# Splitting the first layernorm statistics between ScalarE and VectorE at the start of a fused attention and MLP kernel

## The chip, the cores and the metric

The kernel runs on one core of one Trainium2 chip. The metric is the device time of the whole program in microseconds (us), the median of several runs. All ratios below are the mean time of one kernel's fast runs over the mean of the other's fast runs of the same rounds, so they are not quite the ratio of the medians that stand beside them. "Span" is the length of the one profiled execution; it is some 2 us shorter than the time of the same run.

## The reference, cut to what matters

Two residual blocks on x of 2048 tokens by 1024 columns, in bf16: a linear-memory attention, then a gated MLP. The change touches only the first line of the first block, for the first 512 tokens.

```python
h  = x + _A_ref(_layernorm(x, axis=-1), A_wq, A_wk, A_wv, A_wo, A_beta)
h2 = h + _B_ref(_layernorm(h, axis=-1), B_w_in, B_w_sp, B_b_sp, B_w_out)

def _layernorm(x, axis=-1, eps=1e-05):
    m = jnp.mean(x, axis=axis, keepdims=True)
    v = jnp.var(x, axis=axis, keepdims=True)
    return (x - m) / jnp.sqrt(v + eps)
# ...
    v = (x @ wv).reshape(B, S, H, Dh) ...   # the first products the kernel makes
```

## The kernel before

The program records every operation with the tiles it reads and writes. A list scheduler in the source then fixes the order on each engine from a rough duration for each operation, and semaphores are set from the dependencies. So each engine's order is static: an instruction that waits for a late load holds up all that stand behind it on its engine (below, 0.59 us on VectorE in the changed kernel).

The start loads four x chunks of 128 tokens (x0 to x3, x0 in two halves of 512 columns) and wv in three pieces. The comments in the cut below are added here. The letters of `LOAD` are the order of issue after x0: x1, x2, rows 0 to 3 of wv's first 512 columns ("a"), rows 4 to 7 of the same ("b"), x3, and the other 512 columns ("h"). "Row" here means one block of 128 rows.

```python
    N_WARM = 11                      # matmuls on zeros, before any data is there
    ON_ACT = (1,)                    # x1's statistics are taken on ScalarE
    LOAD = "12ab3h"
    START = 'T00 t01 v00 v01 v02 v03 t10 T11 v04 v05 v06 v07 v10 v11 v12 v13 v14 T20 T21 v15 ...'
    AFTER = [(1, 1, 5)]
    # ...
    def layernorm_act(src, dst, junk, k):          # x1, all 1024 columns on ScalarE
        nm, ss = MV[k][:, 0:1], MV[k][:, 1:2]
        G.op(ACT, lambda e: e.activation(junk, src, ACTF.Identity, scale=-1.0 / D, accum_out=nm), ...)
        G.op(ACT, lambda e: e.activation(junk, src, ACTF.Square, bias=nm, accum_out=ss), ...)
        act(RS[k][:], ss, ACTF.Sqrt, scale=1.0 / D, bias=EPS[:])
        recip(RS[k][:], RS[k][:])
        ts(dst, src, nm, RS[k][:], ALU.add, ALU.mult)
```

`START` is TensorE's order. `T00` or `t00` turns (transposes on TensorE) the first four column blocks of x0; the evictions of a capital T go to VectorE, those of a small t to ScalarE. `v04` is the product of x0's column block 4 with row 4 of wv, first 512 columns; `u04` the same for the other 512. `v00` to `v03` need only the first piece of wv, "a", and the turn `T00`. `v04` to `v07` need piece "b". x3 is turned by a transposing DMA. `AFTER` is one order constraint more: x1's square pass on ScalarE waits until x0 is normalized.

The softmax here doesn't subtract the row's maximum and nothing guards it: scores larger than these inputs give would overflow.

Of the kernel before, what the change touches and what calls it, by code (L numbers as in the profile page):

```python
# [10 lines left out]
ACTF = mybir.ActivationFunctionType  # L11
ALU = mybir.AluOpType

T = 2048
D = 1024
# [8 lines left out]
LN_EPS = 1e-5  # L24
MEM_EPS = 1e-6

PE, ACT, DVE, POOL, SP = range(5)
# [319 lines left out]
def bass_sequential_preLN__memory_aug_infini_attn__mixer_gmlp__prompt_kernel(  # L347
# [16 lines left out]
    G = _Prog(nc)  # L364
# [13 lines left out]
    def tens(name, shape, dt, off=None):  # L378
        sz = int(np.prod(shape[1:])) * mybir.dt.size(dt)
        if off is None:  # L380
            off = region(sz)
        assert off % 32 == 0 and off + sz <= ARENA, (name, off, sz)
        t = nc.alloc_sbuf_tensor_at(name, list(shape), dt, offset=abase + off)
        G.base[t.name] = off
        return t
# [20 lines left out]
    XIN = [tens("xin%d" % i, [128, D], BF16, R_XIN + i * 2048) for i in range(4)]  # L406
    R_HX = region(8192)
    HX = [tens("hx%d" % i, [128, D], BF16, R_HX + i * 2048) for i in range(4)]
# [15 lines left out]
    G1 = tens("g1", [128, H], F32)  # L424
# [3 lines left out]
    MHALF = tens("mhalf", [128, 1], F32)  # L428
    EPS = tens("eps", [128, 1], F32)
    STATS = [tens("stats%d" % i, [128, 4, 6], F32) for i in range(4)]  # L430
    MV = [tens("mv%d" % i, [128, 4], F32) for i in range(4)]
    RS = [tens("rs%d" % i, [128, 1], F32) for i in range(4)]
# [2 lines left out]


    N_WARM = 11
    ON_ACT = (1,)
    LOAD = "12ab3h"


    START = 'T00 t01 v00 v01 v02 v03 t10 T11 v04 v05 v06 v07 v10 v11 v12 v13 v14 T20 T21 v15 v16 v17 v20 v21 v22 v23 v24 v25 v26 v27 u00 u01 u02 u03 u04 u05 u06 u07 u10 u11 u12 u13 u14 u15 u16 u17 u20 u21 u22 u23 u24 u25 u26 u27 v30 v31 v32 v33 v34 v35 v36 v37'
    AFTER = [(1, 1, 5)]
    PS = nc.alloc_psum_tensor("ps", [128, 8, 512], F32)
    G.psum = PS.name

# [3 lines left out]
    def n_of(ap):  # L450
        return int(np.prod([x[1] for x in list(ap.ap)[1:]]))

    def inps(ap):
        return ap.tensor.name == PS.name
# [15 lines left out]
    def act(o, i, func, scale=1.0, prio=0, bias=None):  # L470
        r = [i] + [x for x in (scale, bias) if x is not None and not isinstance(x, float)]
        kw = {} if bias is None else {"bias": bias}
        G.op(ACT, lambda e: e.activation(o, i, func, scale=scale, **kw), r, [o],  # L473
             ((172 if inps(i) else 224) + n_of(i)) / 1.2 + 26, prio=prio, name=str(func))

    def vcost(o, ins, fast):
        n = n_of(o)
        if any(inps(x) for x in ins):
            return ((n / 2 if ins[0].dtype == BF16 and len(ins) == 1 else n) + 151) / 0.96
        if fast == 1:  # L480
            return (n + 151) / 0.96
        return (n / fast + (268 if fast == 4 else 151)) / 0.96
# [4 lines left out]
    def ts(o, i, s1, s2, op0, op1, fast=4):  # L487
        r = [i] + [s for s in (s1, s2) if not isinstance(s, float)]
        G.op(DVE, lambda e: e.tensor_scalar(o, i, s1, s2, op0, op1), r, [o], vcost(o, [i], fast), name="ts", prio=late[0])  # L489
# [11 lines left out]
    def recip(o, i):  # L501
        G.op(DVE, lambda e: e.reciprocal(o, i), [i], [o], (8 * n_of(o) + 151) / 0.96, name="recip", prio=late[0])  # L502

    def ptt(o, a, b, op):
        G.op(POOL, lambda e: e.tensor_tensor(o, a, b, op), [a, b], [o], 550 if op == ALU.pow else
             200 + 1.8 * n_of(o), name="ptt", prio=late[0])

    def pts1(o, i, s, op):
        G.op(POOL, lambda e: e.tensor_single_scalar(o, i, s, op), [i], [o], 220 if n_of(o) < 8 else 220 + 2.5 * n_of(o), name="pts1", prio=late[0])  # L509
# [14 lines left out]
    def bank():  # L524
        b = bank_set[0][bank_rr[0] % len(bank_set[0])]
        bank_rr[0] += 1
        return PS[:, b, :]
# [12 lines left out]
    def w_half(W, A, h, after=False):  # L540
        dma(W[:, :, h * 512:(h + 1) * 512], A.rearrange("(c p) n -> p c n", p=128)[:, :, h * 512:(h + 1) * 512],
            after=after)
# [16 lines left out]

    ln_rr = [0]  # L560

    def layernorm(src, dst, w, prio=0, start=False):
        late[0] = prio
        k = ln_rr[0] % 4
        ln_rr[0] += 1
        nch = (w + 511) // 512
        cs = w // nch
        for ci in range(nch):
            si, so = src[:, ci * cs:(ci + 1) * cs], STATS[k][:, ci, :]
            G.op(DVE, lambda e, si=si, so=so: e.bn_stats(so, si), [si], [so], (cs + 143) / 0.96, name="bn_stats",  # L570
                 prio=late[0])
        sa, mv = STATS[k][:, 0:nch, :], MV[k][:, 0:2]
        G.op(DVE, lambda e: e.bn_aggr(mv, sa), [sa], [mv], 210, name="bn_aggr", prio=late[0])  # L573
        if start:
            act(RS[k][:], MV[k][:, 1:2], ACTF.Sqrt, bias=EPS[:])
            recip(RS[k][:], RS[k][:])
        else:
            pts1(RS[k][:], MV[k][:, 1:2], LN_EPS, ALU.add)
            ptt(RS[k][:], RS[k][:], MHALF[:], ALU.pow)
        ts(dst, src, MV[k][:, 0:1], RS[k][:], ALU.subtract, ALU.mult)  # L580
        late[0] = 0

    def layernorm_act(src, dst, junk, k):
        nm, ss = MV[k][:, 0:1], MV[k][:, 1:2]
        G.op(ACT, lambda e: e.activation(junk, src, ACTF.Identity, scale=-1.0 / D, accum_out=nm), [src], [junk, nm],  # L585
             1250, name="sum")
        G.op(ACT, lambda e: e.activation(junk, src, ACTF.Square, bias=nm, accum_out=ss), [src, nm], [junk, ss],  # L587
             1250, name="sumsq")
        act(RS[k][:], ss, ACTF.Sqrt, scale=1.0 / D, bias=EPS[:])
        recip(RS[k][:], RS[k][:])  # L590
        ts(dst, src, nm, RS[k][:], ALU.add, ALU.mult)


    NJ = [512, 384, 256, 128]
# [13 lines left out]
    def x_load(tc):  # L608
        dma(XIN[tc % 4][:], x2d[tc * 128:(tc + 1) * 128, :])

    def x_norm(tc):
        layernorm(XIN[tc % 4][:], XIN[tc % 4][:], D, 600)

    def x_turn_pe(tc, h, eng):
        dst = XNT[0][:, :, tc * 128:(tc + 1) * 128]
        bb = bank().bitcast(BF16)
        for i in range(4):
            c = 4 * h + i
            tr(bb[:, i * 128:(i + 1) * 128], XIN[tc][:, c * 128:(c + 1) * 128])
        bv = bb[:, 0:512].rearrange("p (c n) -> p c n", c=4)  # L620
        if eng == DVE:
            late[0] = -200
            copy(dst[:, 4 * h:4 * h + 4, :], bv)
            late[0] = 0
        else:
            act(dst[:, 4 * h:4 * h + 4, :], bv, ACTF.Copy)

    def x_turn(tc):
        s, tcl = divmod(tc, 4)
        dma(XNT[s % 2][:, :, tcl * 128:(tcl + 1) * 128], XIN[tc % 4][:], transpose=True)  # L630
# [164 lines left out]
    for i in range(2):  # L795
        pset(V[i][:, :, :, 32:34], 1.0)
    bank_rr[0] = 0
    first = []
    for tcl in range(4):
        first.append(len(G.ops))  # L800
        if tcl in ON_ACT:
            layernorm_act(XIN[tcl][:], XIN[tcl][:], HX[tcl % 2][:], (tcl + 2) % 4)
        else:
            layernorm(XIN[tcl][:], XIN[tcl][:], D, start=True)
    turned, vb = {}, {}
    x_turn(3)
    w_half(WK, A_wk, 0)
    G.ops[-1].deps.add(first[3] + 5)
    for x in START.split():
        c, i = int(x[1]), int(x[2])  # L810
        if x[0] in "tT":
            x_turn_pe(c, i, DVE if x[0] == "T" else ACT)
            turned[c, i] = len(G.ops) - 1
            continue
        if i == 0:
            vb[x[:2]] = bank()
        b, h = vb[x[:2]], x[0] == "u"
        mm(b[:], XNT[0][:, i, c * 128:(c + 1) * 128], WV[:, i, 512 * h:512 * h + 512], i == 0, i == 7)
        if i == 7:
            act(V[0][:, c, 16 * h:16 * h + 16, 0:32], b.rearrange("p (h d) -> p h d", d=32), ACTF.Copy)  # L820
        if x == "u27":

            G.op(ACT, lambda e: e.activation(G1[:, 0:1], RS[2][:], ACTF.Exp, scale=0.0), [RS[2][:]], [G1[:, 0:1]],
                 1500, name="table")

    for c, k, d in AFTER:
        G.ops[first[c] + k].deps.add(turned[d] if isinstance(d, tuple) else first[d // 10] + d % 10)
    bank_rr[0] = 5
    Pq(0)
    for lo, hi in ((0, 128), (128, 512)):  # L830
        b = bank()
# [10 lines left out]
    for i in range(4):  # L842
        p = slice(32 * i, 32 * i + 32)
# [2 lines left out]
        G.op(DVE, lambda e, o=o: e.memset(o, 1.0), [], [o], 160, name="memset")  # L846
    for tc in range(4, 8):
        x_load(tc)
        G.ops[-1].deps.add(first[3] + 5)
    for tc in range(4, 8):  # L850
        x_norm(tc)
        x_turn(tc)
# [62 lines left out]
    for pair in range(16):  # L915
        a, b = 2 * pair, 2 * pair + 1
# [232 lines left out]
```

## Time and profile before

| | |
|---|---|
| time | 796.82 us median of 3 runs (796.44 to 797.57) |
| span of the profiled run | 794.4 us |
| TensorE busy | 783.0 us, 99% |
| TensorE idle from 6 to 12 us | 0.9 us in two waits |
| TensorE idle from 12.4 to 24.8 us | none |

The prediction shows the lines of these views and how to read them. One view is added here: the chain of work that ended last, cut to the first 14 us. Its first line gives the shares of that stretch by what the chain went through (SPq is the issuing of loads, "issue" is time in which the engine waited for nothing that the profile shows).

```profile
by line: PE ps L327 28.6%; DMA xin<-in_A_x_dram 25.6%; ACT hx L587 8.9%; PE ps L468 7.6%; issue 6.4%; SPq L516 5.8%; ACT hx L585 4.9%; DVE xin L489 4.0%; ACT rs L473 2.2%; DVE rs L502 1.2%
```

The chain starts with the load of an x chunk (x1, issued at 1.71), goes through ScalarE's two passes over it (L585 and L587, `hx` is only the place where the unwanted output goes), the root, the reciprocal and the normalizing instruction, and then into TensorE. It is the chain that the change wants to shorten.

### The profile page before, as it was taken

What the parts mean: (1) busy time and instruction counts of PE and PEld (TensorE: products, weight loads), DVE (VectorE), ACT (ScalarE), POOL (GpSimd) and SP (SyncE); (2) the same over time, 40 slices, a digit from 0 to 9 for tenths busy, and PEclk for the clock granted to TensorE, in tenths of its full rate; (3) what the DMA queues carried; (4) which work ended last, traced back from release to release, by engine and by line L of the source; (5) the groups of instructions that cost most, each with busy time, mean ns of one, the idle gap of its engine ahead of it and who ended that gap; (6) DMA issues with size and microseconds to landing.
All of it is one profiled execution on the core that took longest, in us unless ns stands there. A gap on an engine that the chain in (4) does not pass through costs nothing.

```text
span 794.4 us, 11964 instructions
## 1 busy us (share of the span) xinstructions
PE 783.0 (99%) x5273; PEld 321.3 (40%) x4765; DVE 369.4 (47%) x854; ACT 290.6 (37%) x342; POOL 138.7 (17%) x266
## 2 busy tenths in 40 slices
PE   8999999999999999999999999999999999999998
PEld 3455554555554542341322314443244334424433
DVE  6784687868766686804215051132233223322322
ACT  5778887787778852132323323100000000000000
POOL 0454543444433431200001010000000000000000
PEclk9999999999999999999999999999999999999999
DMA  9756612732333657510000116703310530011001
GB/s 282 190 126 160 147 42 67 147 81 54 74 88 95 160 138 210 157 40 1 1 0 1 33 32 156 183 1 78 109 32 1 119 100 1 0 55 59 0 1 53
DMA packets 129526, 65.02 MB, mean 82 GB/s; under 512 B 96576, under 2 KB 121408, under 8 KB 129472
## 3 DMA queue, kind: packets, MB, share of 16 engines
q1 hardware_dynamic: 129472, 64.25, 32.4%
q8 instruction: 39, 0.64, 0.3%
q14 instruction: 15, 0.12, 0.1%
HBM read 32.51 MB, written 8.39 MB: 51 GB/s over the span
## 4 chain that ended last, share of the span: by engine, by line
PE 96%; DVE 2%; issue 1%; ACT 1%; DMA 0%; POOL 0%; SPq 0%
PE ps L327 78%; PE ps L328 15%; PE ps L464 3%; ACT e L473 0%; DMA xin<-in_A_x_dram 0%; DVE stats L570 0%; DVE xin L489 0%; DVE hx L495 0%; DVE pkt L498 0%; ACT hx L587 0%; PE ps L468 0%; DVE oq L495 0%; SPq L516 0%; DVE v L485 0%; ACT hx L585 0%
## 5 line engine op out<-in xcount | busy, mean ns | idle before, releaser
L327 PE MATMUL ps<-wspT,z 128*128 128x512 bf16 x878 | 193.1, 380 | 0.9
L473 ACT ACTIVATE e<-ps 128x2048 bf16<-128x2048 f32 x80 | 149.8, 1873 | 35.1 <-PE ps L464 35.1
L327 PEld LDWEIGHTS ps<-wspT,z 128*128 128x128 bf16 x896 | 87.6, 98 | 106.5 <-issue 1.0
L473 ACT ACTIVATE z<-ps 128x512 bf16<-128x512 f32 x120 | 63.1, 572 | 145.4 <-PE ps L327 140.5
L495 DVE TENSOR_TENSOR tg<-ps,brow 128x512 bf16<-128x512 f32 x56 | 38.7, 691 | 150.0 <-PE ps L327 119.7
L327 PE MATMUL ps<-hnT,win 128*128 128x512 bf16 x438 | 96.7, 379 | 0.5
L700 POOL TENSOR_SCALAR_AFFINE_SELECT e<-e 128x1024 bf16<-128x1024 bf16 (+1 forms) x80 | 77.3, 966 | 112.3 <-ACT e L473 111.9
L328 PE MATMUL ps<-win,hnT 128*128 128x512 bf16 (+1 forms) x381 | 90.0, 344 | 0.5
L570 DVE BATCH_NORM_STATS2 stats<-z 128x6 f32<-128x448 bf16 x64 | 40.1, 627 | 96.8 <-ACT z L473 95.2
L327 PE MATMUL ps<-wout,y 128*128 128x512 bf16 (+2 forms) x243 | 82.5, 367 | 0.0
L328 PE MATMUL ps<-wout,y 128*128 128x512 bf16 x210 | 79.7, 379 | 0.5
L495 DVE TENSOR_TENSOR hx<-hx,ps 128x512 bf16<-128x512 bf16 (+1 forms) x65 | 42.2, 674 | 77.2 <-PE ps L327 76.8
L327 PEld LDWEIGHTS ps<-hnT,win 128*128 128x128 bf16 x448 | 43.8, 98 | 54.2 <-issue 2.0
L327 PE MATMUL ps<-xnT,wq 128*128 128x512 bf16 x250 | 60.3, 381 | 0.4 <-issue 0.2
L327 PE MATMUL ps<-xnT,wk 128*128 128x512 bf16 (+2 forms) x249 | 57.4, 373 | 2.4 <-DVE ra L502 1.9
L327 PE MATMUL ps<-wv,xnT 128*128 128x512 bf16 x239 | 57.2, 380 | 1.4 <-DMA wv<-in_A_wv_dram 0.5
L327 PE MATMUL ps<-wo,oT 128*128 128x512 bf16 x244 | 57.1, 379 | 0.6
L327 PEld LDWEIGHTS ps<-wout,y 128*128 128x128 bf16 x252 | 24.1, 98 | 72.3 <-issue 69.1
L327 PE MATMUL ps<-win,hnT 128*128 128x512 bf16 x122 | 46.3, 380 | 0.0
L327 PEld LDWEIGHTS ps<-win,hnT 128*128 128x128 bf16 x128 | 12.5, 98 | 81.5 <-issue 80.9
L509 POOL TENSOR_SCALAR rs<-mv 128x1 f32<-128x1 f32 x44 | 10.8, 246 | 192.9 <-DVE mv L573 192.9
L327 PEld LDWEIGHTS ps<-v,e 128*128 128x128 bf16 x1280 | 40.1, 96 | 9.8 <-issue 1.7
(72 smaller groups left out, 635.6 us busy)
## 6 DMA issues: line engine op xcount, KB each, us to landing
win<-in_B_w_in_dram SPq DMA_DIRECT2D x6, 1024.0 KB, 5.4
hx<-in_A_x_dram SPq DMA_DIRECT2D x16, 256.0 KB, 3.2
out_dram<-hx SPq DMA_DIRECT2D x16, 256.0 KB, 2.6
hx<-out_dram SPq DMA_DIRECT2D x16, 256.0 KB, 2.7
out_dram<-hx SPq DMA_DIRECT2D x31, 128.0 KB, 1.7
xin<-in_A_x_dram SPq DMA_DIRECT2D x15, 256.0 KB, 5.0
wout<-in_B_w_out_dram SPq DMA_DIRECT2D x2, 1792.0 KB, 11.1
wq<-in_A_wq_dram SPq DMA_DIRECT2D x2, 1024.0 KB, 8.6
```

The lines of the kernel that those rows point to most:

```text
L327: return e.matmul(out, lhsT, rhs, start=start, stop=stop)
L328: return e.add_instruction(mybir.InstMatmult(name="I-%d" % (1000000 + o.idx), engine=e.engine, ins=[e.lower_ap(rhs), e.lower_ap(lhsT)], ou ...
L464: G.op(PE, lambda e: e.matmul(o, lhsT, rhs, start=True, stop=True, tile_position=(32 * i, 0)), [lhsT, rhs], [o], n / 2.4 if last else 3.5, ...
L473: G.op(ACT, lambda e: e.activation(o, i, func, scale=scale, **kw), r, [o], ((172 if inps(i) else 224) + n_of(i)) / 1.2 + 26, prio=prio, na ...
L495: G.op(DVE, lambda e: e.tensor_tensor(o, a, b, op), [a, b], [o], vcost(o, [a, b], fast), name="tt", prio=late[0])
L509: G.op(POOL, lambda e: e.tensor_single_scalar(o, i, s, op), [i], [o], 220 if n_of(o) < 8 else 220 + 2.5 * n_of(o), name="pts1", prio=late[0])
L570: G.op(DVE, lambda e, si=si, so=so: e.bn_stats(so, si), [si], [so], (cs + 143) / 0.96, name="bn_stats", prio=late[0])
L700: G.op(POOL, lambda e: e.affine_select(d, d, pat, ALU.is_ge, 0.0, base=0, channel_multiplier=-1), [d], [d], 1270 if j else 640, name="mask")
```

## The change

The intent: take the statistics of x0, x1 and x3 on two engines at once. ScalarE takes the first columns (256 of x0, 384 of x1, none of x2, 640 of x3) as one triple (count, mean, sum of squared deviations), VectorE takes the rest with its statistics instruction, which writes such triples, and VectorE's aggregation joins them. The order of turns and products is rearranged with it, and x0's first turn is evicted on ScalarE instead of VectorE.

```diff
-    ON_ACT = (1,)
+    SPLIT = (256, 384, 0, 640)
     LOAD = "12ab3h"
-    START = 'T00 t01 v00 v01 v02 v03 t10 T11 v04 v05 v06 v07 v10 v11 v12 v13 v14 T20 T21 v15 ...'
-    AFTER = [(1, 1, 5)]
+    START = ("t00 t01 v00 v01 v02 v03 t10 T11 v04 v05 v06 v10 v11 v12 v07 v13 T20 v14 v15 T21 v16 ..."
+    AFTER = [((2, 'b0'), (0, 'b1')), ((1, 'b0'), (0, 'ag'))]
 ...
+    def layernorm_first(c, wa):
+        src, st = XIN[c][:], STATS[c].rearrange("p a b -> p (a b)")
+        k = {}
+        if wa:
+            n, m, m2 = st[:, 5:6], st[:, 6:7], st[:, 7:8]
+            a, junk = XIN[c][:, 0:wa], HX[c][:, 0:wa]
+            G.op(POOL, lambda e: e.memset(n, float(wa)), [], [n], 130, name="memset")
+            G.op(ACT, lambda e: e.activation(junk, a, ACTF.Identity, scale=1.0 / wa, accum_out=m), ...)
+            G.op(ACT, lambda e: e.activation(junk, a, ACTF.Square, scale=-1.0, bias=m, accum_out=m2), ...)
+        nch = (D - wa + 511) // 512
+        w = (D - wa) // max(nch, 1)
+        for g in range(nch):
+            si, so = XIN[c][:, wa + g * w:wa + (g + 1) * w], st[:, 8 + 6 * g:14 + 6 * g]
+            G.op(DVE, lambda e, si=si, so=so: e.bn_stats(so, si), ...)
+            k["b%d" % g] = len(G.ops) - 1
+        sa, mv = st[:, 5 if wa else 8:8 + 6 * nch], MV[c][:, 0:2]
+        G.op(DVE, lambda e: e.bn_aggr(mv, sa), [sa], [mv], 210, name="bn_aggr")
+        k["ag"] = len(G.ops) - 1
+        act(RS[c][:], MV[c][:, 1:2], ACTF.Sqrt, bias=EPS[:])
+        recip(RS[c][:], RS[c][:])
+        k["rc"] = len(G.ops) - 1
+        ts(src, src, MV[c][:, 0:1], RS[c][:], ALU.subtract, ALU.mult)
+        k["ts"] = len(G.ops) - 1
+        return k
```

`AFTER` holds extra order constraints: here x2's first piece waits for x0's second piece, and x1's first piece for x0's aggregation. The loads and their order are as before.

More of the change, by code (lines that the diff above doesn't have):

```diff
@@ L437, in bass_sequential_preLN__memory_aug_infini_attn__mixer_gmlp__prompt_kernel @@
     N_WARM = 11
-    ON_ACT = (1,)
+    SPLIT = (256, 384, 0, 640)
     LOAD = "12ab3h"
-    START = 'T00 t01 v00 v01 v02 v03 t10 T11 v04 v05 v06 v07 v10 v11 v12 v13 v14 T20 T21 v15 v16 v17 v20 v21 v22 v23 v24 v25 v26 v27 u00 u01 u02 u03 u04 u05 u06 u07 u10 u11 u12 u13 u14 u15 u16 u17 u20 u21 u22 u23 u24 u25 u26 u27 v30 v31 v32 v33 v34 v35 v36 v37'
-    AFTER = [(1, 1, 5)]
+    START = ("t00 t01 v00 v01 v02 v03 t10 T11 v04 v05 v06 v10 v11 v12 v07 v13 T20 v14 v15 T21 v16 v20 v21 v22 v23 "
+             "v17 v24 u00 v25 u01 u02 u03 v26 u10 u04 v27 u05 u06 u07 u11 u12 u13 u14 u15 u16 u17 u20 u21 u22 u23 "
+             "u24 u25 u26 u27 v30 v31 v32 v33 v34 v35 v36 v37 ")
+    AFTER = [((2, 'b0'), (0, 'b1')), ((1, 'b0'), (0, 'ag'))]
     PS = nc.alloc_psum_tensor("ps", [128, 8, 512], F32)
@@ L560, in bass_sequential_preLN__memory_aug_infini_attn__mixer_gmlp__prompt_kernel, with layernorm @@
     ln_rr = [0]
-    def layernorm(src, dst, w, prio=0, start=False):
+    def layernorm(src, dst, w, prio=0):
         late[0] = prio
@@ L573, in layernorm @@
         G.op(DVE, lambda e: e.bn_aggr(mv, sa), [sa], [mv], 210, name="bn_aggr", prio=late[0])
-        if start:
-            act(RS[k][:], MV[k][:, 1:2], ACTF.Sqrt, bias=EPS[:])
-            recip(RS[k][:], RS[k][:])
-        else:
-            pts1(RS[k][:], MV[k][:, 1:2], LN_EPS, ALU.add)
-            ptt(RS[k][:], RS[k][:], MHALF[:], ALU.pow)
+        pts1(RS[k][:], MV[k][:, 1:2], LN_EPS, ALU.add)
+        ptt(RS[k][:], RS[k][:], MHALF[:], ALU.pow)
         ts(dst, src, MV[k][:, 0:1], RS[k][:], ALU.subtract, ALU.mult)
@@ L581, in layernorm @@
         late[0] = 0
-    def layernorm_act(src, dst, junk, k):
-        nm, ss = MV[k][:, 0:1], MV[k][:, 1:2]
-        G.op(ACT, lambda e: e.activation(junk, src, ACTF.Identity, scale=-1.0 / D, accum_out=nm), [src], [junk, nm],
-             1250, name="sum")
-        G.op(ACT, lambda e: e.activation(junk, src, ACTF.Square, bias=nm, accum_out=ss), [src, nm], [junk, ss],
-             1250, name="sumsq")
-        act(RS[k][:], ss, ACTF.Sqrt, scale=1.0 / D, bias=EPS[:])
-        recip(RS[k][:], RS[k][:])
-        ts(dst, src, nm, RS[k][:], ALU.add, ALU.mult)
+    def layernorm_first(c, wa):
[4 more added lines that the diff above has]
+            a, junk = XIN[c][:, 0:wa], HX[c][:, 0:wa]
+            cost = (224 + wa) / 1.2 + 213
+            G.op(POOL, lambda e: e.memset(n, float(wa)), [], [n], 130, name="memset")
+            G.op(ACT, lambda e: e.activation(junk, a, ACTF.Identity, scale=1.0 / wa, accum_out=m), [a], [junk, m],
+                 cost, name="mean")
+            G.op(ACT, lambda e: e.activation(junk, a, ACTF.Square, scale=-1.0, bias=m, accum_out=m2), [a, m],
+                 [junk, m2], cost, name="sumsq")
+        nch = (D - wa + 511) // 512
+        w = (D - wa) // max(nch, 1)
+        for g in range(nch):
+            si, so = XIN[c][:, wa + g * w:wa + (g + 1) * w], st[:, 8 + 6 * g:14 + 6 * g]
+            G.op(DVE, lambda e, si=si, so=so: e.bn_stats(so, si), [si], [so], (w + 143) / 0.96, name="bn_stats")
+            k["b%d" % g] = len(G.ops) - 1
[8 more added lines that the diff above has]
+        return k
@@ L797, in bass_sequential_preLN__memory_aug_infini_attn__mixer_gmlp__prompt_kernel @@
     bank_rr[0] = 0
-    first = []
-    for tcl in range(4):
-        first.append(len(G.ops))
-        if tcl in ON_ACT:
-            layernorm_act(XIN[tcl][:], XIN[tcl][:], HX[tcl % 2][:], (tcl + 2) % 4)
-        else:
-            layernorm(XIN[tcl][:], XIN[tcl][:], D, start=True)
-    turned, vb = {}, {}
+    done = {}
+    for c in range(4):
+        for x, i in layernorm_first(c, SPLIT[c]).items():
+            done[c, x] = i
+    vb = {}
     x_turn(3)
     w_half(WK, A_wk, 0)
-    G.ops[-1].deps.add(first[3] + 5)
+    G.ops[-1].deps.add(done[3, "ts"])
     for x in START.split():
@@ L812, in bass_sequential_preLN__memory_aug_infini_attn__mixer_gmlp__prompt_kernel @@
             x_turn_pe(c, i, DVE if x[0] == "T" else ACT)
-            turned[c, i] = len(G.ops) - 1
+            done[c, "t%d" % i] = len(G.ops) - 1
             continue
@@ L821, in bass_sequential_preLN__memory_aug_infini_attn__mixer_gmlp__prompt_kernel @@
         if x == "u27":
-            G.op(ACT, lambda e: e.activation(G1[:, 0:1], RS[2][:], ACTF.Exp, scale=0.0), [RS[2][:]], [G1[:, 0:1]],
+            G.op(ACT, lambda e: e.activation(G1[:, 0:1], RS[3][:], ACTF.Exp, scale=0.0), [RS[3][:]], [G1[:, 0:1]],
                  1500, name="table")
-    for c, k, d in AFTER:
-        G.ops[first[c] + k].deps.add(turned[d] if isinstance(d, tuple) else first[d // 10] + d % 10)
+    for x, y in AFTER:
+        G.ops[done[x]].deps.add(done[y])
     bank_rr[0] = 5
@@ L848, in bass_sequential_preLN__memory_aug_infini_attn__mixer_gmlp__prompt_kernel @@
         x_load(tc)
-        G.ops[-1].deps.add(first[3] + 5)
+        G.ops[-1].deps.add(done[3, "ts"])
     for tc in range(4, 8):
```

## The prediction

> **What bounds the kernel now.** I read the page first, then the table of windows, TensorE's own waits, the order of time of the first 16 us for each engine, and the DMA issues with their landings.
>
> The page's first and fourth parts say that TensorE carries the span:
>
> ```profile
> PE 783.0 (99%) x5273; PEld 321.3 (40%) x4765; DVE 369.4 (47%) x854; ACT 290.6 (37%) x342; POOL 138.7 (17%) x266
> ...
> PE 96%; DVE 2%; issue 1%; ACT 1%; DMA 0%; POOL 0%; SPq 0%
> ```
>
> TensorE is idle for 794.4 - 783.0 = 11.4 us in all. The change touches only the layernorm of the first four x chunks, so the windows of the start are what counts (columns: window, its length, then each engine's busy time and count; PE first):
>
> ```profile
> 0.00:6.00 6.00, 4.76 (x12) 0.29 (x3) 4.10 (x8) 2.46 (x4) 1.92 (x10) 1.00 0.64 202
> 6.00:12.00 6.00, 5.08 (x39) 2.84 (x38) 5.25 (x13) 3.95 (x10) 0.00 (x0) 1.00 1.04 348
> 12.40:24.80 12.40, 12.40 (x65) 5.93 (x65) 6.39 (x22) 5.84 (x11) 0.80 (x2) 1.00 0.85 253
> ```
>
> From 12.4 to 24.8 us TensorE is busy all the time. Before that it loses time in three places. Its order of time for the start:
>
> ```profile
> 1.64 4.47 PE L328 MATMUL ps<-zero 128*128 128x512 bf16 x10
> 5.91 1.06 PE L468 MATMUL ps<-ident,xin 128*128 128x128 bf16 x8
> 7.46 1.04 PE L327 MATMUL ps<-wv,xnT 128*128 128x512 bf16 x4 [0.49 <-DMA wv<-in_A_wv_dram]
> 8.90 0.62 PE L468 MATMUL ps<-ident,xin 128*128 128x128 bf16 x8 [0.41 <-DVE xin L489]
> 9.55 2.12 PE L327 MATMUL ps<-wv,xnT 128*128 128x512 bf16 x9
> ```
>
> The eleven warm-up matmuls on zeros end at 5.9. The turns of x0 follow at once. The first four products with wv wait until 7.46 for the first half of wv, and the turns of x1 wait until 8.90 for the normalized x1: 0.90 us of idle in the two waits. From 9.55 on nothing is lost. The view of the weight loads shows a further fact that decides this case:
>
> ```profile
> 9.55 0.55 PEld L327 LDWEIGHTS ps<-wv,xnT 128*128 128x128 bf16 x4 [0.20 <-DMA wv<-in_A_wv_dram]
> ```
>
> So the products at 9.55 (v04 on) are released by the **second half of wv's rows**, not by x1. The DMA view agrees: the issue in the window 3.1 to 3.6 is
>
> ```profile
> wv<-in_A_wv_dram SPq DMA_DIRECT2D x1, 512.0 KB, 6.4
> ```
>
> and 3.14 + 6.4 = 9.5 us. By the same working (issue plus landing) x0's halves are there at 2.99 and about 3.45, x1 at 5.30, x2 at 5.99, wv's first half at 7.44, x3 at about 10.2, the other columns of wv at about 13.2.
>
> **What the Trainium skill says.** "ScalarE: Activation LUTs", section What ACT_TABLE_LOAD costs, gives an ACTIVATE 186 ns + 0.833 ns per column, some 93 ns more for a pointer operand, and about 93 ns of overlap back to back. The trace agrees: the mean pass over 1024 columns took 1057 ns (page: 1039), the square pass with its pointer bias 1147. The page gives no time for the read of the accumulator; the trace has 187 ns after each pass, and start to start the two passes cost 1.18 and 1.28 us.
> "DMA: Bandwidth & Descriptors", section Queues, rings and completion order, says that each DMA engine takes descriptors in ring order. The landings above are in the order of issue, as that would have it. The load order is not changed, so I keep every landing up to 13.2 us.
> "TensorE: Matmul & The Clock Gate", section What's actually happening, says that the array runs at half rate until one busy window of 3413 ns has passed, and that these windows run free of the kernel's start. In the trace the warm-up matmuls start every 0.43 us, the first eight turns every 0.107, and at 7.46 the rate has doubled (0.22 per 512 columns). It comes back as a rival.
>
> **The change part by part.** In the same trace a 512-column statistics instruction takes 692 ns and a 448-column one 627, which is 1.0 ns per column. Estimates from this: 384 columns 0.56 us, 320 columns 0.49. From ScalarE's 1.18 and 1.28 us per pair of instructions, less 0.833 ns per column dropped: 0.54 and 0.64 for 256 columns, 0.65 and 0.75 for 384, 0.86 and 0.96 for 640. The aggregation (0.21), the root (0.29), the reciprocal (0.16) and the normalizing instruction (0.55) stay; some 0.04 lies between two.
>
> *x0.* ScalarE takes columns 0 to 255: 3.00 + 0.54 + 0.64 = 4.18. VectorE's two pieces, 256 to 639 and 640 to 1023, both need the second half of x0, so they start at 3.47 and not at 2.99: 3.47 + 0.59 + 0.59 = 4.65, aggregation to 4.86, root 4.90 to 5.19. Before, the aggregation ended at 4.66. So VectorE does 0.27 us less but begins 0.48 later: x0 is 0.2 **later**. Worse, VectorE's order is fixed by the list scheduler in the source. Following its rules by hand (I take the order from it, no time), x1's first piece is put between x0's aggregation and x0's reciprocal, because it is ready while the root is being taken. On the chip x1 lands at 5.30: piece 5.32 to 5.82, reciprocal to 6.00, normalized x0 at 6.58, where it was 5.76. The first turns then start at 6.63, 0.7 after the warm-ups end. Their eviction goes to ScalarE after its passes on x1 (5.32 + 0.65 + 0.75 = 6.72) and ends near 7.9, so v00 starts at about 7.95 where it was 7.46.
>
> *x1.* VectorE: second piece 6.61 to 7.10, aggregation to 7.34. ScalarE evicts the turn first, root about 7.85 to 8.1; VectorE starts on x2 in this wait (7.37 to 8.06), then reciprocal and normalizing, done at about 8.9. Before it was 8.85. The turns of x1 start at 8.9 to 9.0, take 0.44 and end at 9.35 to 9.45.
>
> *The path.* v04 needs those turns and wv's second half at 9.5: it starts at 9.55 as before. What the first chain loses (0.7 at the turns, 0.5 at v00) ends inside the 0.41 wait and the 0.20 of slack; what the change might win at x1 would end there too. After 9.55 the same matmuls follow in another order. The new order sets v10 to v12 before v07: v10 is at 9.55 + 3 x 0.216 = 10.20, its evicted turn is ready at 9.93. The turns of x2 are at 9.55 + 8 x 0.216 = 11.28; x2 is normalized at about 11.05 (second piece 8.9 to 9.6, aggregation 9.83, a turn's copy to 10.27, reciprocal, 0.55). The first product of the other columns of wv moves up to about 13.7, and these land at 13.2. Each margin is 0.2 to 0.5 us, so no new wait, and no gain either.
>
> *x3.* The passes over 640 columns start at 10.25 and are parted by v0's eviction, so the square pass ends near 12.8 and x3 is normalized at about 14.1, not 13.34. Its transposing DMA, wk and x4 to x7 are issued up to 0.8 later. wk landed at 14.74 + 5.8 = 20.5 and is used at 22.7; the transposed x3 at 17.1, used at 19.5: both stay hidden.
>
> Sum: 0.0 from the start, perhaps +0.1 for turns of x1 that come late, and a few tenths either way where the later engine orders come out otherwise.
>
> **The rivals.**
> (a) *VectorE's relief shows up.* The share of VectorE in 6 to 12 us is high (5.25 of 6), and a shorter x1 chain takes away the 0.41 wait. For it: the wait is there. Against it: 0.20 of weight-load idle on wv straight after. If wv in unprofiled runs lands earlier, up to 0.4 us could be won: 796.4.
> (b) *The clock.* The new idle of 0.7 at 5.9 and another near 7.5 fall in the window in which TensorE earns its full rate. If it fails to, v00 to v03 take 4 x 0.427 and end at 9.7, the eight turns 0.86, and v04 starts at 10.5: +0.9, so 797.7. For it: the rate doubled only between 6.7 and 7.46 although the warm-up began at 1.24. Against it: one idle of 0.49 right there did no harm. I give it a quarter.
> (c) *ScalarE becomes the bound.* Its passes on x3 delay the evictions of v0 and the turns, or x2's root: +0.3 to 1.0. ScalarE was busy 3.95 of 6 us and gets about 1 us more by 12, so mostly absorbed.
>
> **Range and chances.** The whole idle at stake is 0.90 us plus what the clock could cost, 0.1% of the time, and the 2% limit is 15.9 us. Base 796.8; a quarter of +0.9 gives +0.2, a fifth of -0.4 gives -0.1: 796.9. Runs of before spread over 1.1 us, so 796.0 to 798.0.
>
> **What would show it right or wrong.** In the changed profile: x0's first statistics instruction at about 3.45; x1's piece between x0's aggregation and reciprocal; first turns at 6.6; v00 near 7.9; v04 at 9.55 released by wv; TensorE full from there to 24.8; x3 normalized near 14.1. A v04 well before 9.5 or after 9.8 would make the central step wrong; slow matmul spacing (0.43) after 7.5 would mean (b); waits of TensorE on ScalarE between 10 and 14 would mean (c); more than 1 us of change coming from after 25 us would mean that the moved orders matter and I mis-sized them.

## The result and the profile after

The changed kernel took 796.61 us median (795.97 to 798.33, 6 runs) against 796.72 (796.27 to 797.57, 6 runs) before: ratio 1.0000, 95% interval 0.9987 to 1.0012. It is the same. One of 798.33 us had a recorded clock of 0.998.

The page's lines on the engines and on the chain:

```profile
PE 781.7 (98%) x5273; PEld 321.0 (40%) x4765; DVE 369.7 (47%) x855; ACT 292.9 (37%) x351; POOL 138.9 (17%) x269
...
PE 96%; DVE 1%; issue 1%; DMA 1%; ACT 0%; SPq 0%; POOL 0%
```

ScalarE has 2.3 us more work, VectorE as much as before. TensorE shows 1.3 us less busy time for the same instructions; the windows say where that is (window, its length, busy time and count of TensorE, of its weight loads, VectorE, ScalarE, GpSimd):

```profile
0.00:6.00 6.00, 3.94 (x11) 0.10 (x1) 3.75 (x7) 3.40 (x9) 2.02 (x13) 1.00 0.64 181
6.00:12.00 6.00, 4.78 (x38) 2.61 (x39) 5.17 (x14) 4.54 (x13) 0.00 (x0) 1.00 1.04 347
12.40:24.80 12.40, 12.40 (x69) 5.91 (x67) 6.08 (x21) 6.31 (x15) 0.80 (x2) 1.00 0.86 264
```

Most of the lost busy time, 0.82 us, lies before 6 us: in this execution the warm-up matmuls reached the full rate earlier and were done sooner. Another 0.30 lies between 6 and 12, where x0's turns ran at the full rate (0.62 us for the eight, 1.06 before). From 12.4 on TensorE is full again. TensorE's order of time in the start:

```profile
1.64 3.54 PE L328 MATMUL ps<-zero 128*128 128x512 bf16 x10
6.68 0.62 PE L471 MATMUL ps<-ident,xin 128*128 128x128 bf16 x8 [1.51 <-DVE xin L492]
7.77 1.04 PE L327 MATMUL ps<-wv,xnT 128*128 128x512 bf16 x4 [0.47 <-ACT xnT L476]
8.73 0.62 PE L471 MATMUL ps<-ident,xin 128*128 128x128 bf16 x8
9.42 1.90 PE L327 MATMUL ps<-wv,xnT 128*128 128x512 bf16 x8
```

x0's turns start at 6.68 where they started at 5.91, v00 at 7.77 instead of 7.46, x1's turns at 8.73 instead of 8.90, and v04 at 9.42 instead of 9.55. So x0 is 0.8 us later, x1 0.17 earlier, and v04 0.13 earlier. That 0.13 is the landing of wv's piece b, which was issued at 3.13 in both traces and landed 6.2 us later here, 6.4 before; the view of the DMA issues in that moment:

```profile
wv<-in_A_wv_dram SPq DMA_DIRECT2D x1, 512.0 KB, 6.2
```

The weight loads name it as what v04 waited for, and the chain to 14 us now runs through that load instead of through x1:

```profile
9.42 1.41 PEld L327 LDWEIGHTS ps<-wv,xnT 128*128 128x128 bf16 x8 [0.25 <-DMA wv<-in_A_wv_dram]
```

```profile
by line: DMA wv<-in_A_wv_dram 44.6%; PE ps L327 30.1%; SPq L519 15.0%; PE ps L471 3.2%; issue 2.9%
```

The chain through x1 has been shortened, and the load that had already ended 0.2 us after it before the change is what is left.

Why x0 is late stands in VectorE's order of time:

```profile
3.48 1.16 DVE L600 BATCH_NORM_STATS2 stats<-xin 128x6 f32<-128x384 bf16 x2 [0.68 <-DMA xin<-in_A_x_dram]
4.67 0.22 DVE L603 BATCH_NORM_AGGREGATE mv<-stats 128x2 f32<-128x15 f32 x1
5.49 0.49 DVE L600 BATCH_NORM_STATS2 stats<-xin 128x6 f32<-128x320 bf16 x1 [0.59 <-DMA xin<-in_A_x_dram]
5.90 0.14 DVE L505 RECIPROCAL rs<-rs 128x1 f32<-128x1 f32 x1
6.08 0.55 DVE L492 TENSOR_SCALAR xin<-xin,mv,rs 128x1024 bf16<-128x1024 bf16 x1
```

Both pieces of x0 start at 3.48, when its second half has landed. ScalarE's root was ready at 5.22, but VectorE stood in front of x1's first piece, 0.59 us, until x1 landed, and took x0's reciprocal after it.

After the start nothing moved. From 45 us to the end, the windows give TensorE an idle time of 749.40 - 740.79 = 8.61 us before and 749.20 - 740.63 = 8.57 after, although the rearranged start had changed the order on VectorE and GpSimd in the attention.

### The profile page after: what moved, and what is told of

Same layout as the page of the kernel before. It is cut to its first block, busy times and chain, and to the rows that moved or that the text cites. A ratio compares the mean times of both kernels' runs of the same rounds, so it can differ in the third digit from the quotient of the medians.

```text
span 794.2 us, 11981 instructions
## 1 busy us (share of the span) xinstructions
PE 781.7 (98%) x5273; PEld 321.0 (40%) x4765; DVE 369.7 (47%) x855; ACT 292.9 (37%) x351; POOL 138.9 (17%) x269
## 4 chain that ended last, share of the span: by engine, by line
PE 96%; DVE 1%; issue 1%; DMA 1%; ACT 0%; SPq 0%; POOL 0%
PE ps L327 78%; PE ps L328 15%; PE ps L467 3%; DMA wv<-in_A_wv_dram 1%; ACT e L476 0%; SPq L519 0%; DVE stats L573 0%; DVE hx L498 0%; DVE xin L492 0%; DVE oq L498 0%; DVE pkt L501 0%; POOL e L719 0%; POOL ra L508 0%; DVE qk L488 0%; DVE hx L492 0%
```

## The experiments

Theory: the start is released at v04 by the landing of piece b, and the span is that release plus a fixed remainder. Rivals: the gain at x1 was eaten by the later x0; VectorE's load bounds the start; the array's clock; the order of turns. All kernels below are the changed kernel with the edit shown, unless it says otherwise. All gave the reference's result within its tolerance.

One table serves all of them. It is from the profiled execution of each kernel; landings are issue plus time to landing. "Turns" is when the first turn of x1 started; a star marks where TensorE was busy with v00 to v03 until then and did not wait for x1.

| kernel | x1 landed | x1's turns | piece b landed | v04 | span | span - v04 |
|---|---|---|---|---|---|---|
| before | 5.3 | 8.90 | 9.5 | 9.55 | 794.4 | 784.85 |
| after | 5.4 | 8.73 | 9.4 | 9.42 | 794.2 | 784.78 |
| after, again (e10) | 5.2 | 8.43 | 9.5 | 9.53 | 794.3 | 784.77 |
| x0 first (e1) | 4.9 | 9.04 | 9.4 | 9.50 | 794.4 | 784.90 |
| VectorE only (e2) | 4.6 | 8.26 | 8.9 | 9.02 | 793.8 | 784.78 |
| old order (e4) | 5.1 | 8.70* | 9.9 | 9.98 | 794.8 | 784.82 |
| x1 longer (e6) | 5.1 | 10.14 | 8.8 | 10.60 | 795.4 | 784.80 |
| finer wv (e7) | 5.3 | 8.64* | in two | 9.09 | 793.9 | 784.81 |
| finer wv, again (e11) | 5.4 | 8.99* | in two | 9.43 | 794.3 | 784.87 |
| after, no wait for b (e8) | 5.2 | 8.90* | not used | 9.35 | 794.1 | 784.75 |
| before, no wait for b (e12) | 4.9 | 8.59 | not used | 9.04 | 793.9 | 784.86 |
| before, no wait for b (e9) | 5.0 | 8.62 | not used | 9.08 | 795.4 | 786.32 |
| no warm-up (e5) | 5.2 | 9.63* | 9.3 | 10.48 | 796.2 | 785.72 |

The last column is the finding. In eleven of thirteen traces, with the products in three orders and the statistics in five arrangements, the span is v04's start plus 784.75 to 784.90 us. Where it is not (e9 and e5), TensorE visibly lost time after v04. Each row is one execution; the runs that were only timed don't show where v04 lay.

**e1, x0 first.**

```diff
-    AFTER = [((2, 'b0'), (0, 'b1')), ((1, 'b0'), (0, 'ag'))]
+    AFTER = [((2, 'b0'), (0, 'b1')), ((1, 'b0'), (0, 'rc'))]
```

> The changed kernel with one order constraint more: x1's first statistics piece waits for x0's reciprocal, so that x0 is not held up by x1's landing. My theory (the products from v04 on are released by the second half of wv's rows, landing at 9.4 to 9.5 us, and all that comes before has slack): the first turns move from 6.68 to about 6.05, v00 from 7.77 to about 7.5, x1's turns stay at 8.7, v04 stays at 9.4 to 9.55, the span stays within 0.3 us of 794.2 and the time is the same. Rival (the gain of the split was eaten by the later x0): v04 would move forward by up to 0.6 us and the span with it.

Measured: 796.36 us against 796.26 (ratio 1.0002, 0.9985 to 1.0019), span 794.4, v04 at 9.50. The order on VectorE was as meant, x0's reciprocal ahead of x1's pieces, but the profiled execution did not show the early turns: x0's second half itself landed 0.6 us later than in the trace after.

```profile
4.08 1.16 DVE L600 BATCH_NORM_STATS2 stats<-xin 128x6 f32<-128x384 bf16 x2 [1.28 <-DMA xin<-in_A_x_dram]
```

The turns came at 6.66, and because VectorE now did x0 first, x1's turns at 9.04; they ended together with b's landing at 9.4. So this trace can't show what an early x0 does. The finer load (e7) has the same constraint with x0 on time: there x0's turns started at 5.91, right behind the warm-ups, against 6.68. Against the rival speaks that v04 stood within 0.1 us of b's landing here as after, which leaves nothing for an earlier x0 to win; the times of this run, with an interval of some 1.4 us to either side, could not exclude 0.6 us by themselves.

**e2, VectorE only.**

```diff
-    SPLIT = (256, 384, 0, 640)
+    SPLIT = (0, 0, 0, 0)
```

> The changed kernel with no column on ScalarE: all statistics of x0 to x3 on VectorE. My theory: x1's chain gets 0.4 to 0.5 us longer than in the changed kernel (two pieces of 512 columns for two of 320), its turns start near 9.2, use up the 0.25 us of slack before wv's second half and end after it: v04 at about 9.7, span +0.25 us to about 794.5, time the same within the noise. Rival (VectorE's load in the start is what bounds): at least the 1 us of VectorE work put back shows, +1 us or more.

Measured: 795.69 us against 796.26 by the medians (ratio 1.0002, 0.9980 to 1.0024; of four runs three were at 795.5 to 795.8 and one at 799.34, at a full clock, unexplained). v04 started at 9.02, not at 9.7:

```profile
9.02 1.41 PEld L327 LDWEIGHTS ps<-wv,xnT 128*128 128x128 bf16 x8 [0.31 <-DMA wv<-in_A_wv_dram]
```

My number missed because I had taken the landings of the trace after; here all loads came earlier. x1's chain, from landing to the first turn, took 8.25 - 4.6 = 3.65 us, within 0.1 of what I had reckoned, but b landed 4.3 us after x1 and not 3.9. So with no ScalarE help at all the start was still released by b. VectorE's load as the bound falls: 1.5 us of its work put back (2 x 0.69 for 2 x 0.56 at x0, for 2 x 0.49 at x1, for 0.56 at x3) cost nothing.

**e6, x1's chain made longer.**

```diff
+        if c == 1:
+            for g in range(2):
+                si, so = XIN[c][:, 512 * g:512 * g + 512], PKT[0][:, 16 * g:16 * g + 12].bitcast(F32)
+                G.op(DVE, lambda e, si=si, so=so: e.bn_stats(so, si), [si, RS[c][:]], [so], 1.0, name="extra")
+                extra = len(G.ops) - 1
         recip(RS[c][:], RS[c][:])
+        if c == 1:
+            G.ops[-1].deps.add(extra)
```

> The changed kernel with two statistics instructions of 512 columns, whose results nobody uses, between x1's root and x1's reciprocal (the scheduler also puts x2's second piece there): about 3 x 0.72 = 2.1 us more in x1's chain, all loads as they were. My theory: the chain has 0.25 us of slack before wv's second half, so v04 moves from 9.42 to about 11.3 and the span grows by 1.8 to 2.1 us, to about 796.1: a dose that goes through one to one once the slack is used. Rival (x1's chain is off the path altogether): under 0.5 us.

Measured: 797.80 us against 796.26, ratio 1.0022 (1.0005 to 1.0039), which includes a run of 799.99 at a recorded clock of 0.996; span 795.4.

```profile
10.14 0.62 PE L471 MATMUL ps<-ident,xin 128*128 128x128 bf16 x8 [1.71 <-DVE xin L492]
10.60 1.89 PE L327 MATMUL ps<-wv,xnT 128*128 128x512 bf16 x8
```

v04 started 1.8 us after b's landing at 8.8, now released by x1's turns. The chain from x1's landing to its first turn took 10.14 - 5.1 = 5.0 us where it takes 3.3, so the dose was 1.75 and not the 2.1 that I had reckoned, and x1 landed 0.3 earlier; both together put v04 at 10.6 and not at 11.3. The span grew by what the chain was over the load, one to one. So the chain is not off the path: it is a path with slack, and the dose has to use up the slack first.

**e5, no warm-up.**

```diff
-    N_WARM = 11
+    N_WARM = 1
```

> The changed kernel with 1 warm-up matmul instead of 11, to measure the clock rival by itself: TensorE is idle until the first turns at 6.68 and does them, v00 to v03 and the next turns at half rate. Expected: v00 to v03 take 4 x 0.427, the turns of x1 0.86, v04 near 10.5[...], span +1.1 to +2.6 us (about 796). If the rate does not matter (all in slack): under 0.3 us.

Measured: 797.93 us against 796.26, ratio 1.0021 (1.0006 to 1.0035), span 796.2. The turns and v00 to v03 ran at half rate:

```profile
7.97 1.86 PE L327 MATMUL ps<-wv,xnT 128*128 128x512 bf16 x4 [0.48 <-ACT rs L476]
9.63 1.06 PE L471 MATMUL ps<-ident,xin 128*128 128x128 bf16 x8
10.48 2.81 PE L327 MATMUL ps<-wv,xnT 128*128 128x512 bf16 x8
```

Four products took 1.86 us (1.04 in the other traces), the turns 0.85 to the next start, v04 came 1.2 us after b, and the first four or five products after it were slow too, which is the 0.9 us by which the last column differs. So the clock cost 1.7 us by the times of this run (2.0 from span to span of the traces, within the +1.1 to +2.6 expected), shown here for an array that was idle for nearly all of the first 6 us.

**e4, the old order of turns and products.** `START` as in the kernel before, the split kept.

> The changed kernel with the order of turns and products of the kernel before; only the split of the statistics stays. My theory: the products from v04 on start about 0.05 us after wv's second half has landed, and the span is that start plus 784.8 us, as in all kernels so far that had a full clock by then (before 9.55 and 794.4, after 9.42 and 794.2, x0 first 9.50 and 794.4, VectorE only 9.02 and 793.8, x1 longer 10.60 and 795.4): v04 at 9.0 to 9.6, span 793.8 to 794.4, time the same. Rival (the new order itself is worth something that the later x0 ate): a span more than 0.3 us longer than v04's start plus 784.8.

Measured: 796.16 us against 796.21, ratio 0.9997 (0.9982 to 1.0013), span 794.8. Piece b landed at 9.9 in this execution, later than expected, and v04 waited for it:

```profile
9.98 2.12 PE L327 MATMUL ps<-wv,xnT 128*128 128x512 bf16 x9 [0.67 <-DMA wv<-in_A_wv_dram]
```

Span less v04 is 784.82 as with the new order. The rearrangement is worth nothing that a trace shows.

**e8, e9 and e12, no wait for piece b (wrong).** The products of x0 and x1 use rows 0 to 3 of wv twice, so that the wait is really gone and not merely left out. The output still passed the tolerance, so passing says little about these products.

```diff
+        r = i % 4 if x[0] == "v" and c < 2 else i
-        mm(b[:], XNT[0][:, i, c * 128:(c + 1) * 128], WV[:, i, 512 * h:512 * h + 512], i == 0, i == 7)
+        mm(b[:], XNT[0][:, i, c * 128:(c + 1) * 128], WV[:, r, 512 * h:512 * h + 512], i == 0, i == 7)
```

e8 is the changed kernel with this edit, e9 the kernel before with it. These two and e12 are single runs, and the record calls their state unknown (the clock reads 1.0 in each).

> Wrong result on purpose: the changed kernel, where the products of x0's and x1's first halves of columns use rows 0 to 3 of wv twice, so that no product before x2's needs the second half of wv. My theory: the next bound is x1's chain: v04 follows the turns of x1 at once, 0.44 us after they start, about 3.7 us after x1's landing (near 9.2 with x1 at 5.46), and the span is v04 plus 784.8 again.

> The same wrong-on-purpose edit in the kernel before. My theory: v04 follows x1's turns, about 4.05 us after x1's landing (near 9.35 with x1 at 5.30). The difference to the changed kernel with the same edit, counted from x1's landing, is what the change would be worth if wv were not the bound: about 0.3 us, 0.04%. Rival (VectorE bounds the start): more than 1 us of difference.

e8: v04 at 9.35, straight after the turns. These did not wait for x1 (normalized at 8.42) but for v00 to v03, because piece a landed late, at 7.95. So the expected 3.7 us from x1's landing to v04 did not come out (9.35 - 5.2 = 4.1), and no trace shows the changed kernel winning by itself what is reckoned below: here b, at 9.2, would have been in time anyway. e9: v04 at 9.08, which is 4.07 after x1's landing, as expected. But its span was 1.5 us too long, and TensorE says why, with one wait of 1.37 us:

```profile
13.65 2.55 PE L327 MATMUL ps<-wv,xnT 128*128 128x512 bf16 x11 [1.37 <-DVE xnT L485]
```

x2's turns were done at 11.6, but VectorE had x3's statistics in front of their evictions, and x3 landed at 11.6 instead of 10.2 in this execution (b at 10.8). So I ran it again:

> The kernel before without the wait on wv's second half (wrong on purpose) once more: in its first run wv's second half and x3 landed 1.3 us late, and VectorE held x2's turns up behind x3's statistics. My theory: with x3 on time, v04 is again 4.05 us after x1's landing and the span is v04 plus 784.8, with no wait of TensorE on VectorE's copies; if the wait for copies is there with x3 on time, the order of VectorE is a bound of its own.

e12: with x3 there at 9.8, v04 came at 9.04, about 4.1 after x1's landing, the span was 793.9, and no wait for the evictions was left.

```profile
8.59 0.62 PE L468 MATMUL ps<-ident,xin 128*128 128x128 bf16 x8 [0.47 <-DVE xin L489]
9.04 2.11 PE L327 MATMUL ps<-wv,xnT 128*128 128x512 bf16 x9
```

These runs size what the change is worth by itself. From x1's landing to its turns being possible, the kernel before takes 3.6 to 3.7 us (8.90 - 5.3, 8.62 - 5.0, 8.59 - 4.9); VectorE alone 3.65; the split 3.2 to 3.3 (8.73 - 5.4, 8.43 - 5.2 and, from x1's normalizing at 8.42 and the 0.05 us to a first turn, e8's 8.47 - 5.2). The turns add 0.44. So the split takes 0.3 to 0.4 us off a chain of 4.05 us. In the eleven traces that load b in one piece, b landed 3.7 to 5.8 us after x1, and in eight of them more than 4.05 us. There what the split saves is wholly hidden by the load; in the other three (after 3.9, e6 3.7, e8 4.0) the split could win between 0.05 and 0.35 us.

**e10 and e11, and e7: a version that starts sooner.** Piece b is loaded as two quarters, "c" (rows 4 and 5) and "d" (rows 6 and 7), so that v04 and v05 need only the earlier one; x0 first as in e1; the turns of x2 a little later.

```diff
-    LOAD = "12ab3h"
+    LOAD = "12acd3h"
-    START = ("... t10 T11 v04 v05 v06 v10 v11 v12 v07 v13 T20 v14 v15 T21 v16 v20 ..."
+    START = ("... t10 T11 v04 v05 v06 v07 v10 v11 v12 v13 v14 v15 T20 v16 T21 v17 v20 ..."
-    AFTER = [((2, 'b0'), (0, 'b1')), ((1, 'b0'), (0, 'ag'))]
+    AFTER = [((2, 'b0'), (0, 'b1')), ((1, 'b0'), (0, 'rc'))]
```

> A try to win what the theory leaves: the second half of wv's rows is loaded as two quarters, x1's first piece waits for x0's reciprocal, and the turns of x2 come two products later. v04 and v05 then need only the third quarter, which lands about 0.7 us before the fourth, and x1's turns, which end near 9.1. My theory: v04 near 9.1, v06 released by the fourth quarter at 9.4 to 9.5, full from there: 0.3 to 0.45 us less span, relative to the landing of the last quarter; 0.05% of the time, which 5 rounds don't resolve. Rival (x1's chain binds): v04 waits for the turns and nothing is gained.

> The changed kernel once more, unedited, beside the finer load on the same chip. My theory: a ratio to the kernel before of 1.000 within 0.1%; in the trace the span is v04's start plus 784.8, and v04 starts 0.05 us after the landing of wv's second half, wherever that falls (so far 8.95 to 9.93).

> The finer load of wv once more, unedited, beside the changed kernel. My theory: 0.4 to 0.7 us under the kernel before and the changed kernel, 0.05 to 0.09%, most likely again not resolved by one call, but together with the first call perhaps; v04 again before the fourth quarter lands. Rival (the 0.56 us of the first call was chance): as often over as under.

e7 took 795.65 us against 796.21 before, ratio 0.9992 (0.9980 to 1.0005); e11, the same kernel, 795.70 against 796.26, ratio 0.9993 (0.9980 to 1.0005); e10, the changed kernel beside e11, 796.52, ratio 1.0002 (0.9989 to 1.0016). In e7's trace

```profile
7.77 1.04 PE L327 MATMUL ps<-wv,xnT 128*128 128x512 bf16 x4 [1.16 <-DMA wv<-in_A_wv_dram]
8.64 0.61 PE L471 MATMUL ps<-ident,xin 128*128 128x128 bf16 x8
9.09 2.32 PE L327 MATMUL ps<-wv,xnT 128*128 128x512 bf16 x10
```

TensorE waits once after x0's turns, for piece a, and then runs without a gap through v00, the turns of x1 and v04. Two details went otherwise than expected: v06 was to be released by the last quarter, but that landed at 9.26 and TensorE did not wait for it; and in e11 v04 started at 9.43, just as that quarter landed and no earlier than in the trace after, because piece a had landed at 8.1. So only e7's trace shows the earlier start. The parts were not run singly; from the 4.05 us of the kernel before, an estimate for its statistics with the finer load in e7 is 5.3 + 4.05 = 9.35 instead of 9.09, so the split would have some part in the gain.

Neither resolves the gain by itself. Over both, the ten runs average 795.71 us (795.29 to 796.24) and eighteen runs of the kernel before 796.24 (795.53 to 796.85): 0.5 us, 0.07%. It is the only version here that is likely to be faster than both kernels (the changed kernel averages 796.46 in e10's five runs), though its cause is seen in one trace of two, and it is far below what counts as a difference.

## Why the prediction was right

The forecast was 796.9 us (796.0 to 798.0), same; the measured median 796.61 lies in the range. That alone says little: the runs of the kernel before spread over 1.3 us, and v04 could have moved by half a microsecond either way without these times showing it. The two small odds in the sum, +0.2 for the clock and -0.1 for VectorE's relief, did not show in the profiled execution. That the clock did no harm there was in part luck: the rate happened to double near 4.2 us, in the trace before only after 6.65. What tests the prediction are its steps:

- **What bounds the start.** Right, and the step that decided: v04 is released by piece b. Expected at 9.55, it came at 9.42, because b landed 0.13 us earlier. The traces show it from both sides: where x1's turns were done before b (before, after, e2, e4, e10), v04 follows b within 0.1 us; where they were later (e6), it follows them.
- **x0 gets later.** Right, mechanism and size. VectorE's pieces started at 3.48 (3.47 expected), x1's piece stood between aggregation and reciprocal, x0 was normalized at 6.63 (6.58), its turns started at 6.68 (6.63). v00 came at 7.77, not 7.95: I had reckoned the turns at half rate, and in this execution they ran at the full one.
- **x1.** I expected 8.9 for its normalized chunk, no earlier than before; it was 8.67, and the turns started at 8.73. The term that was too long is ScalarE's eviction of x0's turn, which ended 0.2 us sooner for the reason just given and let the root start at 7.61. So the one thing that the change itself does for x1, 0.3 to 0.4 us from landing to turns, the prediction had at nought; the error did not matter, because b came later still.
- **x3 later, nothing lost.** Right: x3 was normalized at 13.89 (14.1 expected, 13.34 before). TensorE had no wait for ScalarE between 10 and 14 us and was full from 12.4 to 24.8.
- **Rival (a), VectorE's relief shows up.** It falls, but for a rest. What counts is not an early b but a small distance from x1's landing to b's: in e2 b was early (8.9) and x1 with it (4.6). The distance was under 4.05 us in three of eleven traces, by 0.35 at most, and no timing resolves that.
- **Rival (b), the clock.** It did not strike in the trace after. There the ten warm-ups took 3.54 us, so at 0.427 and 0.216 us a start some six were slow, and the rate doubled near 1.64 + 6 x 0.427 = 4.2, long before the idle. Nor in e1, where the warm-ups were slow to their end, an idle of 0.55 us followed, and the turns behind it ran at full rate. Its cost was mis-sized: I put v04 at 10.5, as e5 measured it (10.48), but left out that the products behind it are slow as well, another 0.9 us. Whether it struck in some unprofiled run of the changed kernel is open, since a time alone doesn't show it; the run of 798.33 and e2's of 799.34 are not explained.
- **Rival (c), ScalarE becomes the bound.** It falls: ScalarE was busy 4.54 of the 6 us, 0.6 more than before.
- **The orders later on.** I allowed a few tenths either way. The fixed remainder of 784.75 to 784.90 us shows that they are worth less than 0.15.

## What to carry to other kernels

Before shortening a chain, look for the one that ends just after it: here one idle of 0.20 us on the weight loads, put down to a load, said in advance that 0.4 us off the statistics would be worth nothing in that execution. With static orders, read which instruction stands in front of the one you speed up: an early piece of the next chunk can hold up the last step of this one until a load lands. And where loads move by half a microsecond from run to run, compare intervals between a landing and what it releases, and not absolute times; start plus a constant remainder is a sharper test than timings that spread over 1 us.

## What the Trainium skill lacked or had wrong

- "ScalarE: Activation LUTs" gives an ACTIVATE's time but none for an accumulator output. The traces show a separate read of 187 ns after each pass, at 256, 384, 640 and 1024 columns alike; start to start a pass with a read costs 0.54 us at 256 columns and 1.18 at 1024. The page's formula for the pass itself holds (416 ns measured at 256 columns, 399 by the formula).
- "VectorE: DVE Perf Modes" has no row for the statistics instructions. Measured, bf16 in SBUF: 489 ns at 320 columns, 559 at 384, 627 at 448, 692 at 512, so about 1.05 ns a column; the aggregation 195 to 222 ns for 9 to 15 values.
- "TensorE: Matmul & The Clock Gate", section What you observe, puts the change of rate around 4 us of sustained activity, give or take 0.5 us from run to run. That is too narrow for these traces: with the same eleven matmuls in front, it came some 3 us after the first matmul in the trace after (near 4.2, as worked out above, less 1.24) and between 5.4 and 6.2 us after it in the trace before (6.66 and 7.46, less 1.24). The page itself also says that the number of slow matmuls differs much between runs of one kernel, and these two traces go with that: some seven of the eleven in the trace after, all eleven in the trace before.
- "DMA: Bandwidth & Descriptors", section Latency and other measured facts, has an HBM latency of 0.2 us on average and 2 us at high load, but does not say how far the landing of one load moves from one execution to the next. The same 512 KB load, issued at 3.12 to 3.13 us in every trace that loads piece b whole, landed between 8.8 and 9.9 us, and once at 10.8; x1's landing moved from 4.6 to 5.4.
